# Splitting k into high and low parts: two doubled writes by ScalarE and GpSimd in place of two VectorE copies

## The chip, the cores and the metric

The kernel runs on one core of one Trainium2 chip. The time is device time in microseconds (us) of one execution, as a median over several executions. Five engines work side by side, each through its own queue of instructions in order: TensorE (PE; its weight loads are listed as PEld), VectorE (DVE), ScalarE (ACT), GpSimd (POOL) and SyncE (SP), which here only issues DMAs. They wait for one another by semaphores.

## The reference

Attention over q, k and v with RMS-normed q and k, then a gated MLP over the heads laid side by side. Batch 8, 12 heads, 448 tokens, head dimension 64; all float32.

```python
def rmsnorm(x, g):
    rms = np.sqrt(np.mean(x * x, axis=-1, keepdims=True) + 1e-06)
    return x / rms * g
q_n, k_n = (rmsnorm(q, g_q), rmsnorm(k, g_k))
scores = 1.0 / np.sqrt(q.shape[-1]) * np.matmul(q_n, k_n.transpose(0, 1, 3, 2))
scores = scores - np.max(scores, axis=-1, keepdims=True)
attn = np.exp(scores)
attn = attn / (np.sum(attn, axis=-1, keepdims=True) + 1e-09)
x = np.matmul(attn, v)                     # then [batch, token, 12 * 64]
h = gelu(x @ w_in)                         # d_ff 1024, tanh form
u, v = h[..., :512], h[..., 512:]
v_s = einsum('ts,bsd->btd', w_sg, layernorm(v) * g_ln) + b_sg[None, :, None]
out = x + (u * v_s) @ w_out
```

## The kernel before

Heads are taken two at a time: 48 pairs, six to a batch. A pair's 896 tokens lie in 7 columns of 128 partitions, so its q and k together are the tile `qk` of 128 x 14 x 64 in float32, q in the first 7 columns (`C7` is 7) and k in the last 7 (`SSW` is 14).

TensorE multiplies in float16, and the float32 precision is kept by splitting each value into a high part (the value rounded to float16) and a low part (the value less the high part). For the scores, q's two parts are stacked along the contracted dimension: 64 high rows and 64 low rows. One matmul of 128 rows against k's parts stacked as (high, low) gives high x high + low x low, and a second against (low, high) gives the two mixed products; PSUM adds both. So the tile `hl` of 21 columns with 2 x 64 values each holds, in 7 columns each, q as (high, low), k as (high, low) and k as (low, high). A DMA transpose on SP's queue (L352) turns `hl` into `qt`, whose columns the scores' matmuls read (L411).

Per pair the steps are these. `squares` (ScalarE L324, VectorE L325) sums squares, for two pairs at a time; `norms` turns them into inverse roots on VectorE. `split` (L341) multiplies k by the two gains (L344) and q and k by the inverse roots (L345) on GpSimd, makes all high parts in one ScalarE activation of 14 columns (L347) and all low parts in one GpSimd subtraction of 14 columns (L348). Two VectorE copies of 7 columns each (L350, L351) then fill the last third of `hl` from the middle third with its halves exchanged. The first pair's split runs on VectorE instead of GpSimd.

`scores` (L395) takes the 7 tiles of a pair's rows: four to six matmuls into PSUM (`s`), the negated maximum on VectorE (L414, `nm`), the exponential with its sum on ScalarE (L416, `a`), the reciprocal of the sums on VectorE (L420, L422, `rc`), then the weights' high part on GpSimd (L430) for three tiles of seven and on ScalarE (L432) for the others, and the low part on VectorE (L433). Both go into `ahl`, which DMA transposes on SP's queue bring into `at` (L436). `pv` multiplies these with v's parts (`vh`, `vl`, made at L384 and L386) and splits the result again (`xh`, `xl`, L461 and L462). The MLP (`moe`) of a batch runs between the pairs of the next batches on all engines; its GpSimd work are L611, L614 and L615.

The source order of instructions is woven from these generators, a few steps of each in turn. The Tile framework then sets each engine's order by priorities and its own timeline estimate of the program, so that a change of one instruction can move others on every engine. Each engine executes its queue strictly in that order. `hl` shares two buffers (tag `t4`) with the squares' scratch tiles; `qt` has two buffers, `a` and `ahl` four each.

Of the kernel before, what the change touches and what calls it, by code (L numbers as in the profile page):

```python
# [13 lines left out]
AF = mybir.ActivationFunctionType  # L14
ALU = mybir.AluOpType
# [5 lines left out]
LEAST_SQ = (1.125 * 2.0 ** -15) ** 2  # L21
ASC = 2.0 ** 14

# places in the order of the work that the MLP and its gelus are moved by
MOFF, MOFF0, GP = 200, 100, 350
# steps of the weights and of the MLP per pair of heads (first, second, middle, last batch)
WR, M0, M1, MR, ML = 3, 8, 7, 11, 11
# pairs of heads at which the first MLP begins and by which the weights are done
I0, WD = 5, 6
# tiles of the scores that share a reciprocal; that are transposed together; whose high part GpSimd  # L30
# makes (in the first batch)
RG = ((0, 2), (2, 4), (4, 7))
TG = (2, 2, 2, 1)
PT, PT0 = (0, 3, 6), (0, 2, 4, 6)
# buffers
NS, NV, NM = 4, 1, 3
NQK, NVR, GV, RAWB = 2, 2, 3, 3
NA, NAH, NAT, NQT, NVH, HLB = 4, 4, 2, 2, 2, 2
# [6 lines left out]
def kernel(  # L45
# [15 lines left out]
    B, H, S, D = q.shape  # L61
    P = 128
# [11 lines left out]
    C7 = 2 * CM + 1  # L74
# [14 lines left out]
    V, A, G = nc.vector, nc.scalar, nc.gpsimd  # L89
    mm = nc.tensor.matmul  # L90

# [1 line left out]
    ones = const.tile([P, P], F32, name="ones")  # L93
    G.memset(ones, 1.0)
    ident = const.tile([P, P], BF16, name="ident")
# [8 lines left out]
    SSW = 2 * C7  # L104
# [3 lines left out]
        V.tensor_scalar(out=y.bitcast(I32), in0=s_i, scalar1=-1, scalar2=MAGIC, op0=ALU.mult, op1=ALU.add)  # L108

    def newton(y, x, t):  # L110
        """y, a guess of x ** -0.5 within 3.5%, made better by a step of third and one of second order."""
        V.tensor_tensor(out=t, in0=x, in1=y, op=ALU.mult)
        V.tensor_tensor(out=t, in0=t, in1=y, op=ALU.mult)
        V.scalar_tensor_tensor(out=t, in0=t, scalar=-10.0 / 3.0, in1=t, op0=ALU.add, op1=ALU.mult)
        V.scalar_tensor_tensor(out=y, in0=t, scalar=5.0, in1=y, op0=ALU.add, op1=ALU.mult)
        V.scalar_tensor_tensor(out=t, in0=x, scalar=-0.5 * 0.375 ** 3, in1=y, op0=ALU.mult, op1=ALU.mult)
        V.tensor_tensor(out=t, in0=t, in1=y, op=ALU.mult)
        V.scalar_tensor_tensor(out=y, in0=t, scalar=1.5 * 0.375, in1=y, op0=ALU.add, op1=ALU.mult)  # L118

    def pow2_scale(name, part, pool):  # L120
        """part [rows, n] holds sums of squares. Gives the power of two that takes
        every element of the tensor below 2^14 * 1.04, and its inverse."""
        rows, n = part.shape
        ps = ps_m.tile([P, 512], F32, name="psc", tag="mm")
        mm(out=ps[:, 0:n], lhsT=ones[0:rows, :], rhs=part, start=True, stop=True)
        x = pool.tile([P, 1], F32, name=name + "_x")
        V.tensor_reduce(out=x, in_=ps[:, 0:n], axis=AX.X, op=ALU.add)
        V.tensor_scalar(out=x, in0=x, scalar1=1e-30, scalar2=None, op0=ALU.max)
        si = pool.tile([P, 1], I32, name=name + "_i")
        sc = pool.tile([P, 1], F32, name=name + "_s")  # L130
        inv = pool.tile([P, 1], F32, name=name + "_v")
        rsqrt_guess(sc, si, x)
        V.tensor_scalar(out=sc.bitcast(I32), in0=sc.bitcast(I32), scalar1=EXPMASK, scalar2=None, op0=ALU.bitwise_and)
        V.tensor_scalar(out=sc, in0=sc, scalar1=ASC, scalar2=None, op0=ALU.mult)
        V.tensor_scalar(out=inv.bitcast(I32), in0=sc.bitcast(I32), scalar1=-1, scalar2=POW2INV, op0=ALU.mult, op1=ALU.add)
        return sc, inv

# [1 line left out]
    W = {}  # L139

    def decode(dst, raw, tmp):
        """float64 words (low, high) to float32; magnitudes below float32's normal range give 0."""
        hi, lo = raw[:, :, 1], raw[:, :, 0]
        di = dst.bitcast(I32)
        V.tensor_scalar(out=di, in0=hi, scalar1=3, scalar2=0x3FFFFFF8, op0=ALU.logical_shift_left, op1=ALU.bitwise_and)
        V.scalar_tensor_tensor(out=di, in0=hi, scalar=-0x40000000, in1=di, op0=ALU.bitwise_and, op1=ALU.bitwise_or)
        V.scalar_tensor_tensor(out=di, in0=lo, scalar=29, in1=di, op0=ALU.logical_shift_right, op1=ALU.bitwise_or)
        hf = raw.bitcast(F32)[:, :, 1]
        A.activation(out=tmp, in_=hf, func=AF.Square)
        G.tensor_scalar(out=tmp, in0=tmp, scalar1=LEAST_SQ, scalar2=None, op0=ALU.is_ge)  # L150
        G.tensor_tensor(out=dst, in0=dst, in1=tmp, op=ALU.mult)

    def weights():
        nonlocal mlp
        ctx_w = ExitStack()
        # w_in's parts take the place of its float32 values, one K block after the other
        wi = const.tile([P, KT, 2, DF], F16, name="wi")
        wi_f = wi.rearrange("p t x f -> p t (x f)").bitcast(F32)
        ws_h = const.tile([P, CK, S], F16, name="ws_h")
# [5 lines left out]
        part = const.tile([P, 2 * KT], F32, name="wi_part")  # L165
# [34 lines left out]
        W.update(ws_h=ws_h, ws_l=ws_l, wo_h=wo_h, wo_l=wo_l, gw=gw, bb=bb)  # L200
        yield

        # w_sg with its rows and columns in the order of the tokens on chip, and the
        # last 64 columns twice, so that both halves of the partitions get them
        wsr = [mlp.tile([P, S], F32, name="wsr", tag="ug", bufs=5) for c in range(CK)]
        for c in range(CM):
            nc.sync.dma_start(out=wsr[c], in_=w_sg[0:SM].rearrange("(p c) s -> p c s", c=CM)[:, c])
# [44 lines left out]
        V.tensor_copy(out=bb[:, SM:S], in_=br[:, SM:S])  # L252
        W["done"] = True

# [1 line left out]
    # A head's tokens on chip: 128 c + p is token 3 p + c for c < 3 (blocks m0, m1, m2), 384 + p the  # L256
    # tail t. A pair of heads A, B is 7 columns of 128 rows: A's m0, m1, m2, then the tails of A and B
    # in one, then B's m0, m1, m2; so A's keys are in the order (m0, m1, m2, t), B's in (t, m0, m1, m2).
    R = {}

    def load_qk(i, qs=None):
# [27 lines left out]
    VR = {}  # L289

    def load_v(i):
        """A head's v in 7 columns: m0, m1, m2, (t, m0a), (m0b, m1a), (m1b, m2a), (m2b, t), with a and b
        the halves of a block: what meets the blocks of A's transposed weights and, from (t, m0a) on, of B's."""
        if i >= NI:
            return
        b, g = divmod(i, NP)
# [12 lines left out]
            VR[i + j] = vr[:, 2 * j:2 * j + 2].rearrange("p h c d -> p (h c d)")  # L309

    def v8(x):
        """Of a pair's columns A's 0..3 and B's 3..6."""
        return bass.AP(tensor=x.tensor, offset=x.offset, ap=[list(x.ap[0]), [10 * D, 2], [1, 4 * D]])

    SS = {}
# [25 lines left out]
    def split(i, E=G):  # L341
        r = R[i]
        qk = r["qk"]
        E.tensor_tensor(out=qk[:, C7:], in0=qk[:, C7:], in1=gg.unsqueeze(1).broadcast_to([P, C7, D]), op=ALU.mult)  # L344
        E.tensor_tensor(out=qk, in0=qk, in1=r["rs"].unsqueeze(2).broadcast_to([P, SSW, D]), op=ALU.mult)  # L345
        hl = prep.tile([P, 3 * C7, 2, D], F16, name="hl", tag="t4", bufs=HLB)
        A.activation(out=hl[:, 0:SSW, 0], in_=qk, func=AF.Copy)  # L347
        E.tensor_tensor(out=hl[:, 0:SSW, 1], in0=qk, in1=hl[:, 0:SSW, 0], op=ALU.subtract)  # L348
        qt = att.tile([P, 3 * C7, P], F16, name="qt", bufs=NQT)
        V.tensor_copy(out=hl[:, SSW:, 0], in_=hl[:, C7:SSW, 1])  # L350
        V.tensor_copy(out=hl[:, SSW:, 1], in_=hl[:, C7:SSW, 0])  # L351
        r["tr"] = nc.sync.dma_start_transpose(out=qt, in_=hl.rearrange("p c x d -> p (c x d)"))  # L352
        r.update(qt=qt.rearrange("p c n -> p (c n)"))

    VS = {}

    def vsquares(i):
        """The sums of squares of the GV pairs of heads from i on."""
        if i >= NI:
            return  # L360
        b, g = divmod(i, NP)
# [25 lines left out]
        r.update(vh=vh, vl=vl)  # L387

    def parts_of(t):
        """Tile t of a pair's 896 rows of scores: (rows of the tile, head)."""  # L390
        if t == CM:
            return [(0, HP, 0), (HP, P, 1)]
        return [(0, P, t // CK)]
# [69 lines left out]
        XT[i] = (xh, xl)  # L463
        del R[i]

# [1 line left out]
    def cluster(acts, done):  # L467
        """Gelu activations, one behind the other from when the last one's operand is ready."""
        p = tc.cur_priority
        tc.cur_priority = max(1, p - GP)  # L470
        load = A.preload_act_table(AF.Gelu_apprx_tanh)
# [13 lines left out]
    def moe(b, early=False):  # L485
# [3 lines left out]
        V.tensor_tensor(out=hs, in0=VS[b]["inv"], in1=W["winv"], op=ALU.mult)  # L489
        vg = mlp.tile([P, CM * DH + FH], F32, name="vg", tag="vggh")  # L490
        mv = sml.tile([P, CK, 2], F32, name="mv", bufs=2)
        # the last 64 tokens have the first half of v in the lower partitions, the second in the upper
        tiles = [(slice(t * P, (t + 1) * P), slice(t * DH, (t + 1) * DH)) for t in range(CM)]
        tiles.append((slice(SM, S), slice(CM * DH, CM * DH + FH)))
        # K block by K block while the batch's last heads are still to come, tile by tile otherwise
        steps = [(t, g) for t in (CM, *range(CM)) for g in range(NP)]
        if early:
            steps.sort(key=lambda x: (x[1], x[0]))
# [122 lines left out]
        if b % 2 == 0:  # L621
# [2 lines left out]
                for n in range(2):  # L624
                    V.tensor_copy(out=xt[:, g, n], in_=X[g][n][:, SM:S])
            GT[b] = gth, gtl, xt
        # the last 64 tokens of two batches go together
        for t in range(CM + b % 2):
            ts = slice(t * P, (t + 1) * P)
            ot = mlp.tile([P, DM], F32, name="ot", tag="v" + "hl"[t % 2])  # L630
# [33 lines left out]
        for g in range(NP):  # L664
            del XT[b * NP + g]

# [1 line left out]
    def low(gen, off):  # L668
        """The instructions of a generator, `off` places later in the order."""
        def run():  # L670
            while True:
                p = tc.cur_priority
# [123 lines left out]
```

## Time and profile before

| | before |
|---|---|
| runs, median (lowest, highest) | 1049.12 us (1044.31, 1051.55) of 3 |
| profiled execution, span | 1047.2 us; no other time of this execution is given, and the median of the runs lies 1.9 us above its span |
| PE / DVE / ACT / POOL busy in it | 809.6 / 899.9 / 705.4 / 504.6 us |
| mean granted TensorE clock | 0.903 |

The span runs from the first instruction to the last in one profiled execution. Busy time of an engine counts its instructions from start to end, and with that also time in which a started instruction was held up. A row of a group gives the line, the engine, the operation, what it writes and reads with shapes, the count, then busy us and mean ns, then the idle time of the engine just before these instructions and who ended it. In the view of one line, three durations stand for the shortest, the median and the longest in ns.

### The profile page before, as it was taken

How to read it: one execution, taken by the hardware profiler on the slowest of the kernel's cores; microseconds unless marked ns; L12 is line 12 of the kernel's file. 1: busy time of each engine (PE TensorE's matmuls, PEld its weight loads, DVE VectorE, ACT ScalarE, POOL GpSimd, SP SyncE). 2: the span in 40 equal slices, each digit the busy share in tenths (PEclk: the TensorE clock that was granted, in tenths of full speed). 3: DMA queues.
4: the chain of work that ended last, by engine and by line, in shares of the span. 5: the costliest groups of instructions: out<-in, count | busy, mean ns of one | idle time of the engine just before them, and what ended most of it. 6: DMA issues, size and time to landing. Idle time of an engine off the chain costs nothing. (4 is left out here: it accounts for less than half of the span.)

```text
span 1047.2 us, 17092 instructions
## 1 busy us (share of the span) xinstructions
PE 809.6 (77%) x5652; PEld 447.3 (43%) x5652; DVE 899.9 (86%) x1959; ACT 705.4 (67%) x1418; POOL 504.6 (48%) x435
## 2 busy tenths in 40 slices
PE   0333556757689798888979899887979799799998
PEld 0111222424454346444644357343634365346546
DVE  4999979999789997999979998999889988999430
ACT  2565787676677777677767767587667686877441
POOL 1777745637536463443545372545455443535021
PEclk9666688888899899899999899999989999999999
DMA  5969589685989979996797879994989779838501
GB/s 144 254 174 244 125 179 215 160 185 108 207 180 206 194 156 206 173 217 152 162 213 181 167 149 196 202 211 106 207 190 195 148 166 201 180 89 174 110 1 61
DMA packets 528217, 177.74 MB, mean 170 GB/s; under 512 B 472257, under 2 KB 521985, under 8 KB 528129
## 3 DMA queue, kind: packets, MB, share of 16 engines
q1 hardware_dynamic: 484928, 144.07, 66.6%
q10 hardware_dynamic: 43200, 32.59, 11.3%
q8 instruction: 44, 0.72, 0.3%
q14 instruction: 45, 0.36, 0.1%
HBM read 54.58 MB, written 11.01 MB: 63 GB/s over the span
## 5 line engine op out<-in xcount | busy, mean ns | idle before, releaser
L433 DVE SCALAR_TENSOR_TENSOR ahl<-a,rc,ahl 128x448 f16<-128x448 f32 x336 | 289.6, 886 | 32.1 <-POOL ahl L430 22.0
L416 ACT ACTIVATE a<-s,nm 128x448 f32<-128x448 f32 x336 | 211.0, 630 | 124.7 <-DVE ahl L433 78.0
L411 PE MATMUL s<-qt 128*128 128x448 f16 (+1 forms) x768 | 192.2, 388 | 120.8 <-ACT a L416 63.5
L430 POOL TENSOR_SCALAR ahl<-a,rc 128x448 f16<-128x448 f32 x150 | 117.3, 786 | 230.0 <-DVE rc L422 99.9
L414 DVE TENSOR_REDUCE nm<-s 128x1 f32<-128x448 f32 x336 | 200.2, 610 | 18.5 <-PE s L411 18.0
L432 ACT ACTIVATE ahl<-a,rc 128x448 f16<-128x448 f32 x186 | 118.1, 662 | 61.5 <-DVE rc L422 34.2
L411 PEld LDWEIGHTS <-qt 128*128 128x128 f16 (+1 forms) x768 | 57.2, 105 | 209.2 <-issue 127.8
L345 POOL TENSOR_TENSOR qk<-qk,ny 128x896 f32<-128x896 f32 x47 | 83.2, 1792 | 70.6 <-DVE ny L118 34.4
L348 POOL TENSOR_TENSOR hl<-qk,hl 128x896 f16<-128x896 f32 x47 | 95.7, 2037 | 34.4 <-ACT hl L347 26.3
L453 PE MATMUL pv<-at,vl 128*64 128x384 f16 x384 | 68.2, 368 | 56.7 <-DMA at<-ahl 44.8
L344 POOL TENSOR_TENSOR qk<-qk,gg 128x448 f32<-128x448 f32 x47 | 58.9, 1255 | 77.0 <-ACT sqk L324 76.8
L453 PE MATMUL pv<-at,vh 128*64 128x384 f16 x672 | 91.0, 357 | 0.0
L575 PEld LDWEIGHTS <-wi 128*128 128x128 f16 x576 | 57.4, 102 | 61.8 <-issue 15.9
L455 PE MATMUL pv<-at,vh 128*64 128x64 f16 x672 | 78.7, 202 | 0.0
L611 POOL TENSOR_TENSOR gt<-gt,u 128x448 f32<-128x448 f32 x32 | 39.0, 1221 | 79.0 <-DVE gt L610 59.2
L453 PEld LDWEIGHTS <-vl 128*64 128x64 f16 x384 | 30.7, 118 | 90.0 <-DMA at<-ahl 37.0
L416 ACT ACTIVATION_READ_ACCUMULATOR a<-s,nm 128x1 f32 x336 | 65.9, 196 | 0.0
L325 DVE TENSOR_REDUCE ss<-sqk 128x14 f32<-128x896 f32 x48 | 51.5, 1073 | 15.5 <-ACT sqk L324 15.2
L347 ACT ACTIVATE hl<-qk 128x896 f16<-128x896 f32 x48 | 45.3, 945 | 25.6 <-DMA qk<-in_k_dram 11.4
L324 ACT ACTIVATE sqk<-qk 128x896 f32<-128x896 f32 x48 | 45.3, 944 | 21.7 <-DVE ss L325 11.2
L453 PEld LDWEIGHTS <-vh 128*64 128x64 f16 x672 | 50.2, 120 | 18.6 <-issue 0.8
L420 DVE TENSOR_SCALAR rc<-sums 128x2 f32<-128x2 f32 x144 | 52.1, 364 | 7.1 <-ACT a L416 6.5
(995 smaller groups left out, 2096.0 us busy)
## 6 DMA issues: line engine op xcount, KB each, us to landing
qk<-in_k_dram ACTq DMA_DIRECT2D x48, 192.0 KB, 3.6
vr<-in_v_dram SPq DMA_DIRECT2D x16, 576.0 KB, 4.9
vr<-in_v_dram SPq DMA_DIRECT2D x32, 288.0 KB, 5.9
out_dram<-ot ACTq DMA_DIRECT2D x24, 384.0 KB, 3.8
qk<-in_q_dram ACTq DMA_DIRECT2D x46, 192.0 KB, 3.6
raw<-in_moe_w_in_dram SPq DMA_DIRECT2D x12, 512.0 KB, 4.9
vr<-in_v_dram SPq DMA_DIRECT2D x32, 96.0 KB, 4.9
at<-ahl SPq DMA_TRANSPOSE x192, 3.8
```

The costliest lines, as they stand in the source:

```text
L344: E.tensor_tensor(out=qk[:, C7:], in0=qk[:, C7:], in1=gg.unsqueeze(1).broadcast_to([P, C7, D]), op=ALU.mult)
L345: E.tensor_tensor(out=qk, in0=qk, in1=r["rs"].unsqueeze(2).broadcast_to([P, SSW, D]), op=ALU.mult)
L348: E.tensor_tensor(out=hl[:, 0:SSW, 1], in0=qk, in1=hl[:, 0:SSW, 0], op=ALU.subtract)
L411: mm(out=ps[p0:p1], lhsT=qt[:, t * P + p0:t * P + p1], rhs=qt[:, k0:k0 + S], start=(n == 0), stop=(n == 1))
L414: V.tensor_reduce(out=nm, in_=ps, axis=AX.X, op=ALU.max, negate=True)
L416: A.activation(out=a, in_=ps, func=AF.Exp, bias=nm, accum_out=sums[:, t - t0:t - t0 + 1])
L430: G.tensor_scalar(out=hl[:, 0], in0=a, scalar1=sc, scalar2=1.0, op0=ALU.mult, op1=ALU.mult)
L432: A.activation(out=hl[:, 0], in_=a, func=AF.Copy, scale=sc)
L433: V.scalar_tensor_tensor(out=hl[:, 1], in0=a, scalar=sc, in1=hl[:, 0], op0=ALU.mult, op1=ALU.subtract)
L453: mm(out=o[:, 0:SM].rearrange("p (c n) -> p c n", c=CM), lhsT=w, rhs=at[:, h * CK:h * CK + CM, blk], start=(n == 0), stop=(n == n_s - 1), ...
L455: mm(out=o[:, SM:S], lhsT=w, rhs=at[:, CM, blk, h * HP:(h + 1) * HP], start=False, stop=(n == n_s - 1), skip_group_check=True)
L575: done = mm(out=ps[:, 0:S], lhsT=ww[:, g, f * P:(f + 1) * P], rhs=xx, start=(n == 0), stop=(n == 17))
```

## The change

The last third of `hl` no longer holds k's parts exchanged. Its middle third now holds k as (high, high) and its last third k as (low, low), while q stays (high, low). The first matmul of the scores then gives q's high and low parts times k's high part, the second both times k's low part; the sum is the same four products. The scores' matmuls, the transpose and all shapes are unchanged.

The doubled parts are written directly: `kd` is a view of k's 7 columns in which every column is read twice (a step of 0). ScalarE's activation writes k's high part twice in one instruction of 896 elements, and a second one of 448 elements writes q's high part. GpSimd's subtraction writes k's low part twice in one instruction of 896 elements, and a second one of 448 elements writes q's low part. The two VectorE copies are gone.

```diff
         hl = prep.tile([P, 3 * C7, 2, D], F16, name="hl", tag="t4", bufs=HLB)
-        A.activation(out=hl[:, 0:SSW, 0], in_=qk, func=AF.Copy)
-        E.tensor_tensor(out=hl[:, 0:SSW, 1], in0=qk, in1=hl[:, 0:SSW, 0], op=ALU.subtract)
+        kd = qk[:, C7:].unsqueeze(2).broadcast_to([P, C7, 2, D])
+        A.activation(out=hl[:, C7:SSW], in_=kd, func=AF.Copy)
+        A.activation(out=hl[:, 0:C7, 0], in_=qk[:, 0:C7], func=AF.Copy)
+        E.tensor_tensor(out=hl[:, SSW:], in0=kd, in1=hl[:, C7:SSW], op=ALU.subtract)
+        E.tensor_tensor(out=hl[:, 0:C7, 1], in0=qk[:, 0:C7], in1=hl[:, 0:C7, 0], op=ALU.subtract)
         qt = att.tile([P, 3 * C7, P], F16, name="qt", bufs=NQT)
-        V.tensor_copy(out=hl[:, SSW:, 0], in_=hl[:, C7:SSW, 1])
-        V.tensor_copy(out=hl[:, SSW:, 1], in_=hl[:, C7:SSW, 0])
         r["tr"] = nc.sync.dma_start_transpose(out=qt, in_=hl.rearrange("p c x d -> p (c x d)"))
```

The changed kernel has two lines more here, so that L414, L430 and L433 of before are L416, L432 and L435 in it, L386 is L388, and L462 is L464. Its activations are L349 and L350, its subtractions L351 and L352.

GpSimd's order before, at two neighbouring pairs in the fifth batch (`ahl<-a,rc` are the high parts of the softmax weights):

```order
L345 TENSOR_TENSOR qk<-qk,ny 128x896 x2
L430 TENSOR_SCALAR ahl<-a,rc 128x448
L348 TENSOR_TENSOR hl<-qk,hl 128x14x64
L344 TENSOR_TENSOR qk<-qk,gg 128x448
L430 TENSOR_SCALAR ahl<-a,rc 128x448 x2
L344 TENSOR_TENSOR qk<-qk,gg 128x448
L348 TENSOR_TENSOR hl<-qk,hl 128x14x64
L430 TENSOR_SCALAR ahl<-a,rc 128x448
```

The same two pairs on GpSimd now:

```order
L345 TENSOR_TENSOR qk<-qk,ny 128x896 x2
L432 TENSOR_SCALAR ahl<-a,rc 128x448
L351 TENSOR_TENSOR hl<-qk,hl 128x896
L352 TENSOR_TENSOR hl<-qk,hl 128x7x64
L432 TENSOR_SCALAR ahl<-a,rc 128x448 x2
L344 TENSOR_TENSOR qk<-qk,gg 128x448 x2
L351 TENSOR_TENSOR hl<-qk,hl 128x896
L432 TENSOR_SCALAR ahl<-a,rc 128x448
L352 TENSOR_TENSOR hl<-qk,hl 128x7x64
```

Each pair has one subtraction more, and the high parts of the softmax weights stand right behind the two, or, in the second pair, between them.

VectorE's order before, in the fifth batch (`nm<-s` are the maxima of the scores):

```order
L351 COPY hl<-hl 128x7x64
L414 TENSOR_REDUCE nm<-s 128x1
L433 SCALAR_TENSOR_TENSOR ahl<-a,rc,ahl 128x448 x3
L414 TENSOR_REDUCE nm<-s 128x1 x2
L462 SCALAR_TENSOR_TENSOR xl<-pv,xh 128x448
L350 COPY hl<-hl 128x7x64
L386 SCALAR_TENSOR_TENSOR vl<-vr,v_s,vh 128x512
L420 TENSOR_SCALAR rc<-sums 128x3
L422 RECIPROCAL rc<-rc 128x3
```

The same place on VectorE now:

```order
L435 SCALAR_TENSOR_TENSOR ahl<-a,rc,ahl 128x448 x2
L416 TENSOR_REDUCE nm<-s 128x1 x3
L435 SCALAR_TENSOR_TENSOR ahl<-a,rc,ahl 128x448 x2
L464 SCALAR_TENSOR_TENSOR xl<-pv,xh 128x448
L416 TENSOR_REDUCE nm<-s 128x1
L388 SCALAR_TENSOR_TENSOR vl<-vr,v_s,vh 128x512
L422 TENSOR_SCALAR rc<-sums 128x3
L424 RECIPROCAL rc<-rc 128x3
```

Both copies are gone, and the maxima and low parts stand in another order among themselves.

## The prediction

> **What bounds the kernel now.** I read the page's busy shares first, then busy time by stage, the longest waits, and the chain of waits.
>
> The page's head and its busy shares:
>
> ```profile
> span 1047.2 us, 17092 instructions
> PE 809.6 (77%) x5652; PEld 447.3 (43%) x5652; DVE 899.9 (86%) x1959; ACT 705.4 (67%) x1418; POOL 504.6 (48%) x435
> ```
>
> Busy time by stage (busy us of each engine, its instructions in brackets):
>
> ```profile
> core 0: us, PE busy (x) PEld busy (x) DVE busy (x) ACT busy (x) POOL busy (x), PEclk, DMA share, GB/s
> 100.00:864.00 764.00, 615.36 (x4306) 338.16 (x4305) 699.53 (x1524) 548.47 (x1107) 387.29 (x328) 0.90 0.83 178
> 980.00:1047.20 67.20, 60.02 (x393) 37.35 (x390) 12.34 (x36) 22.33 (x34) 10.07 (x12) 0.99 0.13 37
> ```
>
> From 100 to 864 us VectorE is busy 699.5 of 764 us (92%), ScalarE 72%, GpSimd 51%. The last 67 us are TensorE's and have no split of k in them. So VectorE is the nearest to a bound, in the stage where the change works, but not alone. The waits (total us, times, longest):
>
> ```profile
> PE s L411 <- ACT a L416: 63.5, 40, 7.9
> PE s L411 <- DMA qt<-hl: 51.8, 9, 27.5
> ACT a L416 <- DVE ahl L433: 78.0, 80, 4.7
> DVE ahl L433 <- POOL ahl L430: 22.0, 28, 3.6
> DVE ss L325 <- ACT sqk L324: 15.2, 7, 5.5
> DVE ahl L433 <- ACT ahl L432: 10.1, 9, 2.1
> SPq L352 <- DVE hl L350: 32.3, 12, 5.6
> ```
>
> TensorE's scores wait for the exponentials, whose buffers wait for VectorE's low parts (L433): the loop closes on VectorE. The chain of waits from 893 to 945 us, the last stretch with splits (start, us, what):
>
> ```profile
> by line: DVE ahl L433 12.5%; DVE nm L414 11.3%; issue 6.9%; PE s L411 5.2%; PE ms__11321 L605 5.2%; PE ms__11376 L605 5.0%; DVE hl L351 4.9%; PE ms__11416 L605 4.8%; DVE rc L420 4.5%; DVE st L532 4.1%; DVE ly L108 3.5%; DVE li L107 3.4%; PE
> 894.44 1.93 DVE hl L351
> 900.53 0.20 DVE hl L350
> 908.68 0.20 DVE hl L350
> ```
>
> The copies themselves lie on this chain: L351 with 4.9% of 52 us, 2.55 us, and L350 with at least 0.40.
>
> **What goes: the copies.** Their groups, their shortest, median and longest durations in ns, and their busy time in that same stretch (the row of L351, then that of L350):
>
> ```profile
> L351 DVE COPY hl<-hl 128x448 f16<-128x448 f16 x48 | 25.4, 531 | 0.1
> L350 DVE COPY hl<-hl 128x448 f16<-128x448 f16 x48 | 15.6, 325 | 0.0
> L351 DVE COPY hl<-hl x48: 265/278/1968, 20.7 to 924.8; 128x448 f16<-128x448 f16 x48
> 893.00:945.00 52.00, 2.69 (x4) 1.00 0.59 126
> 893.00:945.00 52.00, 1.11 (x4) 1.00 0.59 126
> ```
>
> VectorE loses 25.4 + 15.6 = 41.0 us of busy time, far over 96 x 0.278 = 26.7 us: the rest is time in which a copy was held up while GpSimd worked. In the stretch 2.55 + 0.40 = 2.95 of 3.80 us, 78%, lay on the chain.
>
> **What GpSimd gains.** The groups that price it (busy us, mean ns):
>
> ```profile
> L348 POOL TENSOR_TENSOR hl<-qk,hl 128x896 f16<-128x896 f32 x47 | 95.7, 2037 | 34.4 <-ACT hl L347 26.3 <-issue 5.8 <-DVE mv L545 1.0
> L345 POOL TENSOR_TENSOR qk<-qk,ny 128x896 f32<-128x896 f32 x47 | 83.2, 1792 | 70.6 <-DVE ny L118 34.4 <-issue 18.3 <-DVE rc L422 7.9
> L344 POOL TENSOR_TENSOR qk<-qk,gg 128x448 f32<-128x448 f32 x47 | 58.9, 1255 | 77.0 <-ACT sqk L324 76.8
> L614 POOL TENSOR_TENSOR gl<-gt,gh 128x448 fp32r<-128x448 f32 x32 | 41.3, 1290 | 1.5 <-ACT gh L612 1.4
> ```
>
> The subtraction of L348 stays one instruction of 896 elements, now 7 columns of k read twice; its own 2.04 us is the nearest row. The repeated operand could make it 1.79 (L345 repeats one) or, read as two of L344, 2.51: -12 to +22 us in 47 pairs. q's low part is a new instruction of 448 elements: half of L348 is 1.02, L344 gives 1.26, L614 1.29. I take 1.15, between the half of its own kind and the whole instructions of that size: 47 x 1.15 = 54 us (48 to 61). GpSimd goes from 48% to 53% of the span. That is hidden where nobody waits for GpSimd; VectorE's wait for GpSimd's high parts is 22.0 us in 504.6 busy, 0.044 per us, so 54 us more bring 2.4 us.
>
> **What GpSimd's time does to VectorE.** Three groups with their shortest, median and longest durations, and their means:
>
> ```profile
> L433 DVE SCALAR_TENSOR_TENSOR ahl<-a,rc,ahl x336: 658/676/2397, 40.9 to 977.9; 128x448 f16<-128x448 f32 x168
> L433 DVE SCALAR_TENSOR_TENSOR ahl<-a,rc,ahl 128x448 f16<-128x448 f32 x336 | 289.6, 886 | 32.1 <-POOL ahl L430 22.0 <-ACT ahl L432 10.1
> L386 DVE SCALAR_TENSOR_TENSOR vl<-vr,v_s,vh x48: 726/742/2366, 58.2 to 969.6; 128x512 f16<-128x512 f32 x48
> L386 DVE SCALAR_TENSOR_TENSOR vl<-vr,v_s,vh 128x512 f16<-128x512 f32 x48 | 47.3, 986 | 0.1
> L420 DVE TENSOR_SCALAR rc<-sums x144: 128/159/1698, 34.3 to 975.5; 128x2 f32<-128x2 f32 x96, 128x3 f32<-128x3 f32 x48
> L420 DVE TENSOR_SCALAR rc<-sums 128x2 f32<-128x2 f32 x144 | 52.1, 364 | 7.1 <-ACT a L416 6.5
> ```
>
> Above their medians they lose 336 x 0.210 = 70.6, 48 x 0.244 = 11.7 and 52.1 - 144 x 0.159 = 29.2 us, together 111.5 us beside 504.6 us of GpSimd: 0.22 us for each us. So 54 us more cost VectorE about 12 (7.6 if L433 alone counts, 0.14 per us; 54 if every added us is met in full). VectorE's net relief is 41 - 12 = 29 us. The Trainium skill (SBUF — State Buffer, section Who interferes with whom) states the mechanism and speaks against this change: a VectorE instruction with two inputs in SBUF and a GpSimd instruction that reads SBUF exclude each other, the later one blocked for the whole of the other. By that rule L433's longest should exceed its shortest by about one GpSimd instruction, and 2397 - 658 = 1739 ns beside L345's 1792 agrees; the sum by the rule at its worst is the third rival below.
>
> **What ScalarE gains.** One activation of 896 elements stays (k twice), one of 448 is new:
>
> ```profile
> L347 ACT ACTIVATE hl<-qk 128x896 f16<-128x896 f32 x48 | 45.3, 945 | 25.6 <-DMA qk<-in_k_dram 11.4 <-DVE ss L325 5.3 <-DMA qt<-hl 4.5
> L612 ACT ACTIVATE gh<-gt 128x448 fp32r<-128x448 f32 x32 | 18.1, 570 | 11.3 <-POOL gt L611 11.3
> L432 ACT ACTIVATE ahl<-a,rc 128x448 f16<-128x448 f32 x186 | 118.1, 662 | 61.5 <-DVE rc L422 34.2 <-issue 11.4 <-DVE nt L116 2.6
> ```
>
> 48 x 0.57 (L612, a copy without a scale; L432, with one, 0.66) = 27 us (to 32): 67% becomes 70%. Its first half is hidden, since GpSimd's subtraction of k waits only for the first activation. What waits for ScalarE: TensorE 63.5 us on exponentials, VectorE 25.3 on L324 and L432, in 705.4 busy: 0.13 per us. 27 us more bring 3.
>
> **What moves.** The transpose of `hl` on SP's queue no longer waits for VectorE (32.3 us in 12 waits for L350, 2.7 each) but for GpSimd's second subtraction, 1.15 us after its first. Behind it in SP's queue stand the transposes of `ahl`. In front of TensorE this counts only where `qt` is late: 51.8 less the first wait of 27.5 leaves 24.3 us in 8 waits. One us less in most of them is possible, and as much more where a high part slips between the two subtractions; I put -1. The first pair runs on VectorE, where a subtraction of 448 takes the place of two copies: nothing.
>
> **The sum.** How much of 29 us comes through? In the one stretch that the chain shows, 78% of the copies lay on it; before that VectorE is 92% busy beside TensorE's 81%, and a second path (TensorE, ScalarE) is right behind. I take 0.6: -17.4, then +3 (ScalarE), +2.4 (GpSimd), -1 (`qt`): -13 us. The profiled span 1047.2 becomes 1034; the median of the runs is 1049.1, 1.9 above that span, so 1036.
>
> **The rivals.** About 1% (10.5 us) is what a measurement of this kernel can tell from no change.
>
> First, *relief that goes nowhere*: VectorE's 29 us turn into waits for scores and exponentials. For it: TensorE waits 63.5 us for ScalarE, which gets 27 us more, and the order of every engine is planned anew, so that other waits appear. Against it: ScalarE itself waits 78.0 us for VectorE. A share of 0.2 instead of 0.6 gives -5.8 + 4.4, 1048; with 0.4, 1042.
>
> Second, on the other side, *high parts queued behind the longer split*. In GpSimd's order L430's `ahl` stands right behind the subtractions; VectorE's L433, and all that is queued behind it, waits for it. If in a pair that wait grows by the whole new 1.15 us, 48 pairs give 55 us, and 41 saved less 12 less 55 leaves VectorE 26 us worse: at 0.6 and with ScalarE's 3, 1049 + 19 = 1068. It decides from 29 / 1.15 = 25 pairs on. Today 28 of 150 high parts are waited for, 9 in 48; so a half-way case, 1055 to 1060, is the likelier form.
>
> Third, *GpSimd's added time met in full by VectorE*: 54 against 41 saved, 13 us worse, and with ScalarE's 3 and GpSimd's 2.4 1061 at 0.6 to 1067. It decides where a us of GpSimd costs VectorE over 41 / 54 = 0.76 us; the rows say 0.22. This is the exclusion rule of the Trainium skill's page SBUF — State Buffer at its worst.
>
> That the copies stay is no rival: VectorE's order has none of them left.
>
> **How the numbers follow.** Forecast (a share of 0.5 to 0.8 comes through) 0.50, first rival 0.31, second 0.13, third 0.06. The forecast's own range: a share of 0.8 with 33 us of relief (0.14 per us) gives 1027, and 1.79 us subtractions a little less; a share of 0.5 gives 1039. The range is 1023 to 1055: it takes in the first rival and the mild form of the second, and leaves out the bad ends of the second and third and some 5% below. Faster by over 1% means below 1038.6: nearly all of the forecast, 0.45. Within 1%: the rest of it and most of the first rival, 0.35. Slower: the other two rivals and a little of the first, 0.20.
>
> **What would show it.** VectorE's busy time about 870 us; L433's mean from 886 to some 910 ns; a new GpSimd group of 448 elements at 1.0 to 1.3 us; ScalarE at about 733 us; VectorE's idle time between 100 and 900 us no more than some 12 us above before. The forecast is wrong if that idle time grows by most of the relief (first rival), if VectorE's wait for `ahl` of L430's line goes from 22 to over 50 us (second), or if L433's mean passes 1.0 us (third).

## The result, and the profile after

The changed kernel takes 1077.63 us (median of 4 runs, 1075.86 to 1079.03) against 1048.15 us (median of 4, 1044.31 to 1051.55) of the kernel before on the same chip: a ratio of 1.0286 with a 95% interval of 1.026 to 1.0312. It is 2.9% slower. The forecast was 1036 us, and the range ended at 1055. One execution of e4 and one of e15 below took about 2570 us and are left out of the times and ratios given for them.

The profiled execution of the changed kernel, its head and its busy shares:

```profile
span 1076.9 us, 17030 instructions
PE 820.6 (76%) x5652; PEld 449.0 (42%) x5652; DVE 911.9 (85%) x1864; ACT 724.7 (67%) x1466; POOL 561.4 (52%) x482
```

VectorE has lost 95 instructions and is still busy for 911.9 us, 12 more than before (899.9). GpSimd has 47 instructions and 56.8 us more, ScalarE 48 instructions and 19.3 us more.

The groups of the split and of the softmax weights' low part (`L435` was `L433`), and the durations of `L435` one by one (shortest, median, longest):

```profile
L435 DVE SCALAR_TENSOR_TENSOR ahl<-a,rc,ahl 128x448 f16<-128x448 f32 x336 | 316.9, 968 | 24.8 <-POOL ahl L432 13.8 <-ACT ahl L434 10.9
L351 POOL TENSOR_TENSOR hl<-qk,hl 128x896 f16<-128x896 f32 x47 | 94.7, 2016 | 45.9 <-ACT hl L349 35.6 <-issue 4.9 <-DVE vg L562 2.7
L352 POOL TENSOR_TENSOR hl<-qk,hl 128x448 f16<-128x448 f32 x47 | 58.4, 1244 | 0.0
L350 ACT ACTIVATE hl<-qk 128x448 f16<-128x448 f32 x48 | 27.1, 565 | 0.0
L435 DVE SCALAR_TENSOR_TENSOR ahl<-a,rc,ahl x336: 659/680/2405, 34.4 to 1007.3; 128x448 f16<-128x448 f32 x168
```

The new instructions cost what they were thought to cost: 1.24 us on GpSimd, 0.57 us on ScalarE, and the subtraction that reads k twice takes 2.02 us, as the old one did (2.04). But `L435` has gone from 886 to 968 ns in the mean. Its median is as before (680 against 676) and so is its longest; more of the 336 are held up. That alone is 27.3 us.

How they are held up shows in the order of time (start and duration in us; two of VectorE's low parts, then GpSimd's new subtraction):

```profile
687.44 1.52 DVE L435 SCALAR_TENSOR_TENSOR ahl<-a,rc,ahl 128x448 f16<-128x448 f32 x1
688.96 0.68 DVE L435 SCALAR_TENSOR_TENSOR ahl<-a,rc,ahl 128x448 f16<-128x448 f32 x1
687.45 1.03 POOL L352 TENSOR_TENSOR hl<-qk,hl 128x448 f16<-128x448 f32 x1
```

The first low part begins together with the subtraction and ends 0.48 us after it; the second has the usual length. 125 of the 336 take at least 60 ns more than the median, 99 before. All but one of these (four before) end 0.47 to 0.49 us after the end of some GpSimd instruction. 17 begin while the new subtraction `L352` runs, or up to 60 ns ahead of it, and all 17 take 1.08 us or more.

The longest waits after, and the busy time of each engine in the stage that answers to 100 to 864 us of before:

```profile
DVE nm L416 <- PE s L413: 32.3, 30, 7.4
DVE ahl L435 <- POOL ahl L432: 13.8, 18, 1.4
ACT a L418 <- DVE ahl L435: 92.4, 88, 4.0
PE s L413 <- ACT a L418: 59.4, 38, 5.4
PE s L413 <- DMA qt<-hl: 46.2, 12, 25.2
100.00:893.00 793.00, 622.61 (x4294) 337.08 (x4293) 713.60 (x1446) 565.86 (x1150) 433.69 (x369) 0.89 0.80 170
```

The stage has become 29 us longer, which is nearly the whole loss. VectorE is busy 713.6 us in it, 14.1 more than before, and idle 79.4 us against 64.5, 14.9 more. So the loss has two halves: VectorE's instructions are longer, and it waits more, above all for scores (`nm`, 18.0 to 32.3 us). Its wait for GpSimd's high parts has fallen from 22.0 to 13.8 us.

### The profile page after: what moved, and what is told of

It is laid out like the page before. It is cut to its first block, busy times and chain, and to the rows that moved or that the text cites. A ratio compares the mean times of both kernels' runs of the same rounds, so it can differ in the third digit from the quotient of the medians.

```text
span 1076.9 us, 17030 instructions
## 1 busy us (share of the span) xinstructions
PE 820.6 (76%) x5652; PEld 449.0 (42%) x5652; DVE 911.9 (85%) x1864; ACT 724.7 (67%) x1466; POOL 561.4 (52%) x482
## 5 line engine op out<-in xcount | busy, mean ns | idle before, releaser
L435 DVE SCALAR_TENSOR_TENSOR ahl<-a,rc,ahl 128x448 f16<-128x448 f32 x336 | 316.9, 968 | 24.8 <-POOL ahl L432 13.8
L432 POOL TENSOR_SCALAR ahl<-a,rc 128x448 f16<-128x448 f32 x150 | 115.2, 772 | 219.8 <-DVE rc L424 91.9
L416 DVE TENSOR_REDUCE nm<-s 128x1 f32<-128x448 f32 x336 | 199.9, 611 | 32.8 <-PE s L413 32.3
L351 POOL TENSOR_TENSOR hl<-qk,hl 128x896 f16<-128x896 f32 x47 | 94.7, 2016 | 45.9 <-ACT hl L349 35.6
L418 ACT ACTIVATION_READ_ACCUMULATOR a<-s,nm 128x1 f32 x336 | 66.6, 198 | 0.0
L349 ACT ACTIVATE hl<-qk 128x896 f16<-128x896 f32 x48 | 45.4, 946 | 26.0 <-DMA qk<-in_q_dram 11.7
L352 POOL TENSOR_TENSOR hl<-qk,hl 128x448 f16<-128x448 f32 x47 | 58.4, 1244 | 0.0
```

The costliest lines, as they stand in the source:

```text
L351: E.tensor_tensor(out=hl[:, SSW:], in0=kd, in1=hl[:, C7:SSW], op=ALU.subtract)
L352: E.tensor_tensor(out=hl[:, 0:C7, 1], in0=qk[:, 0:C7], in1=hl[:, 0:C7, 0], op=ALU.subtract)
L416: V.tensor_reduce(out=nm, in_=ps, axis=AX.X, op=ALU.max, negate=True)
L418: A.activation(out=a, in_=ps, func=AF.Exp, bias=nm, accum_out=sums[:, t - t0:t - t0 + 1])
L432: G.tensor_scalar(out=hl[:, 0], in0=a, scalar1=sc, scalar2=1.0, op0=ALU.mult, op1=ALU.mult)
L435: V.scalar_tensor_tensor(out=hl[:, 1], in0=a, scalar=sc, in1=hl[:, 0], op0=ALU.mult, op1=ALU.subtract)
```

## The experiments

The trace after mixes two things, since the planner gave every engine a new order. Two causes were to be told apart: that GpSimd's new work holds up VectorE by more than the copies had cost it, and that the new order alone makes the loss. In the kernels called "in the order of before" every engine's queue is held to that order by dependencies that only order one engine's instructions; an instruction that before lacks stands directly behind its neighbour in the split. One run below (e17) holds the order, moves the tiles by 512 bytes and has otherwise the work of before; it takes the same time, 0.9995 [0.9969, 1.0021]. The cuts of code leave out what notes an instruction's place for the order, and the guard that keeps the first pair, which VectorE splits, free of additions on GpSimd.

Each ratio is against the kernel before, run beside the changed one on the same chip (medians 1046.8 to 1048.7 us). A gain or loss in us is worked out from the ratio; a plain difference of the medians can lie some 2 us off it.

### The instructions without the order, and the order without the instructions

e1 is the changed split in the order of before; e2 is the split of before in the order of the changed kernel, in which only the copies' places on VectorE are the planner's.

> The changed split with every engine's order fixed to that of the kernel before: the two activations stand where the one stood, the two subtractions where the one stood, the copies are gone, nothing else moves. Theory A (the added GpSimd time costs VectorE and its queue more than the copies did): 1065 to 1080 us, as the changed kernel, with L433's kind of instruction at about 0.97 us mean. Theory B (the planner's new order costs the time, the instructions themselves save some): 1036 to 1048 us. In between, 1050 to 1062, both have a share.

> The kernel before, with its one activation, one subtraction and two copies, in the changed kernel's order on every engine; only the two copies' places on VectorE are left to the planner. Theory A: 1045 to 1055 us, since GpSimd has no added work. Theory B: 1070 to 1085 us, the changed kernel's order with the copies still to pay.

e1: 1060.8 us, ratio 1.0113 [1.0081, 1.0145]. e2: 1063.3 us, ratio 1.0132 [1.0069, 1.0196]. The two add up to 2.45% of the 2.86%. Each is a loss by itself, and neither cause is the whole. Held against one another at a fixed order, the changed instructions cost 1.13% in the order of before and 1.0286 / 1.0132, 1.5%, in the new one.

Busy shares of e1 and its low parts with the wait for GpSimd's high parts (`L504` and `L501` there), then the low parts of e2 (`L500`):

```profile
PE 811.3 (77%) x5652; PEld 446.7 (42%) x5652; DVE 906.3 (86%) x1864; ACT 724.7 (69%) x1466; POOL 560.8 (53%) x482
L504 DVE SCALAR_TENSOR_TENSOR ahl<-a,rc,ahl 128x448 f16<-128x448 f32 x336 | 309.7, 947 | 30.7 <-POOL ahl L501 21.8 <-ACT ahl L503 8.8
L500 DVE SCALAR_TENSOR_TENSOR ahl<-a,rc,ahl 128x448 f16<-128x448 f32 x336 | 305.6, 934 | 21.1 <-POOL ahl L497 12.7 <-ACT ahl L499 8.0 <-issue 0.2
```

Without any change of order VectorE has 6.4 us more to do than before, where the prediction had 29 less. Its wait for high parts is 21.8 us (22.0 before): VectorE does not wait longer for what is queued up behind the longer split. The low parts grow in both runs, from a mean of 886 to 947 ns in e1 and to 934 in e2, where GpSimd has no work more than before: the order alone also makes more of them meet a GpSimd instruction.

### GpSimd's half alone, ScalarE's half alone

e3 adds to the kernel before, in its order, only the second subtraction; e4 only the second activation. The copies stay in both, and both write again what stands there already.

First e3's edit (for the pairs that GpSimd splits), then e4's:

```diff
         E.tensor_tensor(out=hl[:, 0:SSW, 1], in0=qk, in1=hl[:, 0:SSW, 0], op=ALU.subtract)
+        E.tensor_tensor(out=hl[:, 0:C7, 1], in0=qk[:, 0:C7], in1=hl[:, 0:C7, 0], op=ALU.subtract)
```

```diff
         A.activation(out=hl[:, 0:SSW, 0], in_=qk, func=AF.Copy)
+        A.activation(out=hl[:, 0:C7, 0], in_=qk[:, 0:C7], func=AF.Copy)
```

> The kernel before in its own order, plus one subtraction of 448 elements on GpSimd in 47 pairs (q's low part, written a second time) right behind the one of 896; the copies stay. It prices the GpSimd half alone. Theory A: 1075 to 1095 us (about 57 us of GpSimd time that comes through at 0.5 to 0.8). Theory B: 1048 to 1056 us.

> The kernel before in its own order, plus one activation of 448 elements on ScalarE in each pair (q's high part, written a second time) right behind the one of 896; the copies stay. It prices the ScalarE half alone, 27 us of busy time. Theories A and B both say 1048 to 1053 us; a rival by which ScalarE's time delays the exponentials says 1060 or more.

e3: 1077.3 us, ratio 1.0256 [1.0194, 1.0317], 26.9 us. e4: 1054.8 us, ratio 1.0044 [1.0015, 1.0073], 4.6 us. Of e3, the busy shares, the low parts, the copy that was `L351`, the new subtraction, and VectorE's wait for high parts:

```profile
PE 823.7 (77%) x5652; PEld 451.4 (42%) x5652; DVE 933.5 (87%) x1959; ACT 705.1 (66%) x1418; POOL 561.3 (52%) x482
L507 DVE SCALAR_TENSOR_TENSOR ahl<-a,rc,ahl 128x448 f16<-128x448 f32 x336 | 304.3, 930 | 29.7 <-POOL ahl L504 21.9 <-ACT ahl L506 7.6
L425 DVE COPY hl<-hl 128x448 f16<-128x448 f16 x48 | 31.3, 654 | 0.1
L422 POOL TENSOR_TENSOR hl<-qk,hl 128x448 f16<-128x448 f32 x47 | 58.2, 1239 | 3.7
DVE ahl L507 <- POOL ahl L504: 21.9, 27, 3.9
```

GpSimd's busy time rises by 56.7 us and VectorE's by 33.6 with the same instructions: 0.59 us for each us, where the prediction took 0.22. The low parts gain 14.7 us and the copy 5.9. The time rises by 26.9 us, four fifths of VectorE's 33.6.

### The copies' removal alone

e5 leaves the copies out in the order of before. The last third of `qt` is transposed from the middle third of `hl` by a second DMA, so that scores get plain products in place of the exchanged ones: this part of the computation is left out, at the same number of instructions on TensorE. The second DMA is a cost of its own that e5 contains.

```diff
-        V.tensor_copy(out=hl[:, SSW:, 0], in_=hl[:, C7:SSW, 1])
-        V.tensor_copy(out=hl[:, SSW:, 1], in_=hl[:, C7:SSW, 0])
-        r["tr"] = nc.sync.dma_start_transpose(out=qt, in_=hl.rearrange("p c x d -> p (c x d)"))
+        r["tr"] = nc.sync.dma_start_transpose(out=qt[:, 0:SSW], in_=hl[:, 0:SSW].rearrange("p c x d -> p (c x d)"))
+        nc.sync.dma_start_transpose(out=qt[:, SSW:], in_=hl[:, C7:SSW].rearrange("p c x d -> p (c x d)"))
```

> The kernel before in its own order without the two copies: the last third of qt is transposed from the middle third of hl by a second DMA right behind the first (14 columns, then 7), so k's exchanged products are left out and replaced by the plain ones; everything else is computed as before. It prices the removal alone. By the prediction's account VectorE is freed of 41 us, at a share of 0.6 to 1 1008 to 1024 us. By the account that the earlier runs suggest (the held time of a copy passes to the next instruction, only 96 times 0.278, 27 us, is freed, and nearly all of it counts) 1022 to 1030 us. If VectorE's time didn't bound at all: 1044 to 1052 us.

e5: 1036.3 us, ratio 0.988 [0.9855, 0.9904], 12.6 us gained. It lies in none of the three ranges expected, between "27 us are freed" and "VectorE does not bound". Its busy shares and low parts:

```profile
PE 818.5 (79%) x5652; PEld 447.5 (43%) x5652; DVE 879.0 (85%) x1863; ACT 703.3 (68%) x1418; POOL 504.9 (49%) x435
L502 DVE SCALAR_TENSOR_TENSOR ahl<-a,rc,ahl 128x448 f16<-128x448 f32 x336 | 299.0, 915 | 33.7 <-POOL ahl L499 23.1 <-ACT ahl L501 10.5
```

The copies were 41.0 us, but VectorE's busy time falls by 20.9 only. The low parts, with GpSimd unchanged, become 9.4 us longer: a GpSimd instruction that held up a copy now holds up what stands next. The traces bear this out. If each delay of a VectorE instruction (its time above the median of its group, from 60 ns on) is put down to the GpSimd instruction that ran when it began, the delays behind the split's subtraction are 64.5 us before, with the copies, and 63.1 us in e5, without them. The 12.6 us are 0.60 of the 20.9.

e1 and e5 both lack the copies and differ in what GpSimd and ScalarE got: VectorE is busy 27.3 us more in e1 for 55.9 us of GpSimd, 0.49 for each us, and e1 takes 2.4% longer.

### Is it GpSimd's time, or what it reads?

e6 puts three memsets of 320 elements (1.1 us per pair) on GpSimd behind the subtraction, e7 one subtraction of 320 elements into a scratch tile. Both write only scratch, which nobody waits for, in the 47 pairs that GpSimd splits. First e6's edit, then e7's:

```diff
+        for _ in range(3):
+            G.memset(scr, 0.0)
```

```diff
+        G.tensor_tensor(out=scr.rearrange("p (c d) -> p c d", d=D), in0=qk[:, 0:5], in1=hl[:, 0:5, 0], op=ALU.subtract)
```

> The kernel before in its own order, plus about 1.2 us of GpSimd work per pair that reads nothing from SBUF: three memsets of a small scratch tile in the place of the added subtraction; nobody waits for them. If GpSimd's added time costs through its queue (the softmax weights' high parts behind it), 1065 to 1078 us. If it costs by holding up VectorE's instructions that read two operands, 1046 to 1053 us.

> As the run with the memsets, but with one subtraction of 320 elements that reads q and its high part and writes a scratch tile, so that it reads SBUF and neither the transpose nor anything else waits for it: about 0.9 us in 47 pairs, 42 us. If GpSimd's reads hold up VectorE (0.59 us for each us, as the run with the subtraction of 448 showed), 1064 to 1073 us. If the cost came from the later transpose of hl, 1048 to 1054 us.

e6: ratio 1.0247 [1.0221, 1.0272]; e7: 1.0329 [1.0307, 1.0352]. The memsets cost 2.5% without making VectorE's instructions longer (the mean of the low parts was 882 ns against 886), so that something else was at work. The scratch tile had been put ahead of all others and had moved them by 640 bytes. So e9 and e10 repeat the two with the scratch tile behind the transposed tiles, which then stay where they were, and e11 moves the tiles alone.

> The run with three memsets again, but the scratch tile lies behind the transposed tiles in SBUF, so that none of them moves by 640 bytes as in the first form, where the transposes of ahl took 4.5 us to land instead of 3.8. If GpSimd's added time costs through its queue, still 1065 to 1078 us; if the first form's cost was the shifted tiles and memsets cost nothing, 1047 to 1054 us.

> The run with a scratch subtraction of 320 elements again, with the scratch tile behind the transposed tiles. If GpSimd's reads hold up VectorE, 47 us of GpSimd at 0.59 is 28 us of VectorE, 1064 to 1076 us. If that cost came from the shifted tiles or from the transpose that waits for the subtraction, 1047 to 1055 us.

> The kernel before in its own order with 640 bytes of unused SBUF put ahead of all tiles, written once at the start; no other work. If the shift by 640 bytes slows the transposes as in the first two scratch runs: at<-ahl 4.5 us to landing and 1062 to 1076 us. If not: 1046 to 1052 us.

e9: 1054.4 us, 1.0079 [1.0047, 1.0111]. e10: 1065.3 us, 1.0168 [1.0132, 1.0204]. e11: 1070.1 us, 1.0195 [1.0155, 1.0234]: the place of the tiles was most of e6 and much of e7, and these two runs price nothing else. That e6 fell into the range of the theory that GpSimd's queue costs the time was an accident of that. Busy shares of e9 and one of its memsets, then of e10 and its subtraction:

```profile
PE 812.2 (77%) x5652; PEld 448.9 (43%) x5652; DVE 905.1 (86%) x1959; ACT 703.8 (67%) x1418; POOL 550.9 (52%) x576
L423 POOL MEMSET scr<- 128x320 f16 x47 | 17.3, 368 | 0.0
```

```profile
PE 814.8 (77%) x5652; PEld 447.1 (42%) x5652; DVE 917.7 (87%) x1959; ACT 703.9 (66%) x1418; POOL 548.2 (52%) x482
L423 POOL TENSOR_TENSOR scr<-qk,hl 128x320 f16<-128x320 f32 x47 | 45.8, 974 | 0.0
```

For 46.3 us of writing VectorE's busy time rises by 5.2 us, 0.11 for each us; for 43.6 us of reading and writing by 17.8, 0.41. The Trainium skill (SBUF — State Buffer, section Who interferes with whom) says the same of the kind: a VectorE instruction with two inputs in SBUF contends with a GpSimd instruction that reads SBUF, and not with one that only writes it. It does not say how much of GpSimd's reading falls on VectorE; here it is 0.41 to 0.59. In single instructions the difference is plain; two low parts of e9, one behind the other, and two of the memsets under which they begin:

```profile
371.23 1.27 DVE L510 SCALAR_TENSOR_TENSOR ahl<-a,rc,ahl 128x448 f16<-128x448 f32 x2
370.96 0.36 POOL L423 MEMSET scr<- 128x320 f16 x1
371.81 0.36 POOL L425 MEMSET scr<- 128x320 f16 x1
```

30 low parts of e9 begin under a memset, counted in the same way, and 29 of them take 0.66 to 0.67 us, as if alone; the last was caught by the subtraction behind it. But e9 is still 0.8% slower than before, so up to half of e10's 1.7% need not come from reading. VectorE's wait for high parts is 22.3 us in e9 (22.0 before), so it is not that wait by which the memsets cost time; which path it is stays open.

### What the place of the tiles does

e17 and e18 put 512 and 128 unused bytes ahead of all tiles, in the order of before:

```diff
+    G.memset(const.tile([P, 4 * D], F16, name="pad"), 0.0)
```

(This is e17's; e18 has D, e11 had 5 * D.) With 512 the tiles move by a multiple of 256 bytes; with 128, as with the 640 of e11, by a multiple of 256 and 128 more. That `ahl`, `at` and `qt` stand on multiples of 256 in the kernel before is taken as given; no trace shows an address.

> The kernel before in its own order with 512 bytes of unused SBUF per partition put ahead of all tiles, where 640 cost 1.95%. Theory A, the 640 bytes cost because they moved every tile from a multiple of 256 bytes to one of 128: here all tiles stay on multiples of 256, and the time is 1044 to 1052. Theory B, any shift costs (a draw of where tiles fall against one another): 1058 to 1075.

> The same with 128 bytes. Theory A: the tiles stand off multiples of 256 as with 640 bytes, 1064 to 1074, with the transposes' landing at 4.5 and 6.7 us as there, not 3.8 and 5.7. Theory B: another value than with 640 bytes, 1045 to 1075, with no tie to the landing times.

e17: 1048.7 us, 0.9995 [0.9969, 1.0021]. e18: 1064.4 us, 1.0155 [1.0122, 1.0189]. DMA queue `q1` (its share of the DMA engines' time) and the time to landing of the transposes, in us, first of before, then of e18:

```profile
q1 hardware_dynamic: 484928, 144.07, 66.6%
at<-ahl SPq DMA_TRANSPOSE x192, 3.8
qt<-hl SPq DMA_TRANSPOSE x48, 5.7
```

```profile
q1 hardware_dynamic: 484928, 144.07, 72.8%
at<-ahl SPq DMA_TRANSPOSE x192, 4.5
qt<-hl SPq DMA_TRANSPOSE x48, 6.6
```

The same packets and bytes take longer after a move by 128 bytes off the multiples, and only there: in e17 the transposes land in 3.8 and 5.8 us, in e11 in 4.5 and 6.7. The changed kernel adds no tile, so this has no part in its loss.

### Both copies on ScalarE

e8 gives both copies to ScalarE, in the order of before (the second one's place is left to the planner), and leaves GpSimd's one subtraction as it was; e12 is the same with the planner's own order.

```diff
         A.activation(out=hl[:, 0:SSW, 0], in_=qk, func=AF.Copy)
+        A.activation(out=hl[:, SSW:, 1], in_=qk[:, C7:], func=AF.Copy)
         E.tensor_tensor(out=hl[:, 0:SSW, 1], in0=qk, in1=hl[:, 0:SSW, 0], op=ALU.subtract)
-        V.tensor_copy(out=hl[:, SSW:, 0], in_=hl[:, C7:SSW, 1])
-        V.tensor_copy(out=hl[:, SSW:, 1], in_=hl[:, C7:SSW, 0])
+        A.activation(out=hl[:, SSW:, 0], in_=hl[:, C7:SSW, 1], func=AF.Copy)
```

> The kernel before in its own order, with both copies made by ScalarE (the high part from the float32 k beside the first activation, the low part from the float16 low part, its place left to the planner), GpSimd as before: ScalarE gains 54 us, VectorE loses the copies, GpSimd gains nothing. From the runs before, twice 6 us for ScalarE less 22 to 27 for the copies: 1032 to 1040 us, faster than both kernels. If ScalarE's second half delays qt or the exponentials: 1048 us or more.

> Both copies on ScalarE, with the order left to the planner altogether. In the old order this took 1041 us. If the planner's order for it is as good as the old one, 1038 to 1045 us; if a new order costs as much as the changed kernel's did (1.3%), 1050 to 1058 us.

e8: 1041.0 us, 0.9924 [0.9903, 0.9945]. e12: 1042.2 us, 0.9933 [0.9904, 0.9962]. It is faster than both kernels, in either order. Its busy shares in e8:

```profile
PE 811.2 (78%) x5652; PEld 447.6 (43%) x5652; DVE 880.8 (85%) x1863; ACT 745.3 (72%) x1514; POOL 502.5 (48%) x435
```

VectorE is relieved by 19.1 us as in e5, and ScalarE's 39.9 us more take only part of the gain.

### Is the order luck?

MOFF0, the priority offset of the first batch's MLP, reorders all engines, in the runs below from somewhere between the seventh and the thirteenth pair on, and changes no instruction (100 in both kernels). e13, e14 and e15 are the changed kernel with 80, 110 and 120, e16 the kernel before with 150.

> The changed kernel, one number of the planner altered: the priority offset MOFF0 of the first batch's MLP is 80 instead of 100. That reorders every engine from about the sixth pair on; the instructions are the same. The changed kernel in before's order took 1061, in its own order 1078. Theory A, its own order is one draw of a planner that scatters: another draw lies anywhere between about 1055 and 1080, and the three draws of the changed kernel differ by more than 6 us among themselves. Theory B, the order that the planner must make of these instructions is the worse one (for example since no copies stand between the maxima): all draws lie at 1072 to 1084.

> The same with MOFF0 at 110; the orders part from about the fourth pair on. Theory A: anywhere between 1055 and 1080. Theory B: 1072 to 1084.

> The same with MOFF0 at 120. Theory A: anywhere between 1055 and 1080. Theory B: 1072 to 1084. In neither does a draw fall to before's 1048, since the instructions alone cost 12 us in before's own order.

> The kernel before with MOFF0 at 150 instead of 100, which gives its unchanged instructions another order from the second pair on. Theory A: before's own order was a good draw, another is slower by up to 15 us, 1048 to 1064. Theory B: within 5 us of 1048.

e13: 1077.4 us, 1.0295 [1.0259, 1.033]. e14: 1070.6 us, 1.0222 [1.0196, 1.0248]. e15: 1080.1 us (three runs), 1.032 [1.0287, 1.0353]. e16: 1058.5 us, 1.0097 [1.0066, 1.0127]. Orders of the same instructions scatter by about 1%, as theory A had it: the changed kernel's four own orders lie between 1071 and 1080, and the kernel before, which stood at 1048, stands at 1058 and at 1063 (e2) in two others. Its own order was the best of the three tried. But theory A also allowed the changed kernel 1055 to 1070 in its own orders, and none lies there. Theory B for them, 1072 to 1084, is missed by e14 alone, and by little; for the kernel before, within 5 us of 1048, it is missed by e16. Some of its orders' loss may therefore follow from the change; four and three draws do not tell. Which wait of the new order makes the loss stays open too. In e2 ScalarE's exponentials wait longer for VectorE, 93.6 against 78.0 us, and VectorE longer for scores, 28.0 against 18.0:

```profile
ACT a L483 <- DVE ahl L500: 93.6, 91, 5.3
DVE nm L481 <- PE s L478: 28.0, 27, 5.5
```

But e12, at 1042 us, has 29.5 us of the second as well, and e13, at 1077 us, only 14.4, so that wait is no cause by itself. An order also changes how often VectorE is held up: with the instructions of before VectorE is busy 905.5 us in e2 and 913.1 in e16, against 899.9.

## Why the prediction was wrong, point by point

It was wrong in sign. Two terms of the sum were mis-sized, and one had no price.

- **The copies' relief, 41.0 us.** The step took their busy time, and so also the time in which they were held up, as time that VectorE gets back. Only 20.9 us came back (e5) or 19.1 (e8): the hold passes to the next instruction. The prediction had the better figure beside it, 96 x 0.278 = 26.7 us, and took the other.
- **GpSimd's time, 0.22 us of VectorE for each us, 12 us.** This is the step that failed most. It divided the delays of three of VectorE's groups, 111.5 us, by all of GpSimd's busy time. Measured, the added subtraction cost 0.59 in e3, 33.6 us. The trace before could have said so. The delays of all VectorE's groups, counted as under e5, are 193 us there, 0.38 for each us of GpSimd, and they differ by GpSimd's instruction: 64.5 us behind the 95.7 of `L348` (0.67), the added one's own kind, and 21.9 us behind the 117.3 of `L430` (0.19). The average over all of GpSimd's work hid the price of the one kind that was added. Behind it stood the claim that 0.22 is far from the 0.76 at which the third rival decides; e3's 0.59 is nearer to that than to 0.22. That rival (6%) named the right mechanism and the right side, with L433's mean over 1.0 us as its sign; the mean came to 968 ns, 947 in the order of before, and did not reach the sign. With a relief of 21 us instead of 41 its threshold was not 0.76 but 21 / 54 = 0.39.
- **The share of 0.6 that comes through.** Right for the relief (12.6 of 20.9 us in e5), too small for the burden (26.9 of 33.6 in e3).
- **The size of the new instructions.** Right: 58.4 us on GpSimd (54, with 61 as the upper bound), 27.1 us on ScalarE (27). The ScalarE half cost 4.6 us, where 3 was taken.
- **High parts queued behind the longer split (second rival, 13%).** Refuted by its own sign, over 50 us: VectorE's wait for them is 21.8 us in e1, 21.9 in e3 and 13.8 in the changed kernel.
- **Relief that goes nowhere (first rival, 31%).** There was no relief to lose: VectorE's busy time rose. Its idle time in the stage grew by 14.9 us, little more than the 12 that the forecast allowed.
- **The order.** The prediction said that every order is planned anew and gave it no price. By e2 it costs 13.8 us (interval 7 to 21), nearly half of the loss. The pieces of order that were shown, 8 or 9 lines each, could not show that. The scatter of about 10 us between orders should have stood in the range on both sides, and, as the kernel before had the best order of three, mostly on the slow one.

Put together in the order of before: -12.6 (copies, e5) + 26.9 (GpSimd, e3) + 4.6 (ScalarE, e4) = +18.9 us, against 11.9 measured in e1. The gap of 7 us is within the intervals of the four runs. It may have a reason too: e3 still has the copies, which are held up 5.9 us more in it, and in e1 there are none to hold. With e1's 11.9 and the order's 13.8, 25.7 of the 30 us are accounted for one by one; the rest appears only where both come together.

## What to carry to other kernels

In this kernel, with VectorE busy 86% of the time, a us of added GpSimd subtraction cost 0.4 to 0.6 us of VectorE, and instructions whose mean lay far above their median gave back no more than their median when they were removed (20.9 us of 41.0, with medians of 26.7). Elsewhere both are to be read from the trace by the kind of GpSimd's instruction, not as one average. Work taken from VectorE went well to ScalarE here (0.992) and badly to GpSimd (1.011 at the same order). Before a change of 1% is believed or dropped in a kernel whose order a planner sets, it should be measured in the old order as well, or in several orders.

## What the runs showed of the hardware that was not expected

A tile's address is worth more than half of what the change cost: 128 or 640 unused bytes ahead of all tiles cost 1.55% and 1.95%, 512 bytes nothing (0.9995). The transposes into `at` land in 4.5 us instead of 3.8 where the tiles are moved by 128 bytes off a multiple of 256, plain loads of `vr` (576 KB) in 5.3 instead of 4.9 (e11), at equal packets and bytes. The Trainium skill (DMA: Bandwidth & Descriptors, section How a descriptor splits into AXI transactions) gives a rule that fits: a descriptor's bytes are moved in pieces that start at multiples of 256 bytes, and one that starts between them fetches bytes that it does not use. The share of `q1`, 66.6% on the multiples and 72.8% off them, agrees with it; no run here shows the transactions themselves. The rule speaks of bytes fetched, which fits the transposes' reading of `ahl` and `hl`; the loads of `vr` only write to the tiles that moved, and for them the reason stays open.
